# Attention with four sink columns and a gated MLP on one core: sinks of three tiles held as high, low and high parts in 72 rows of f32r

## The chip, the cores and the metric

One core of a Trainium2 chip runs the whole program. The metric is the device time of one execution in microseconds (us); lower is better. The kernel before was timed three times, and the median is what counts. One execution was also taken by the hardware profiler; its instruction records are "the trace" below.

## The reference

Inputs are q, k and v of shape (4, 8, 768, 64) in float32 (batch, heads, sequence, head dimension), four sinks, a window of 128 keys, and the weights of an MLP with 512 inputs and 1024 hidden columns. The attention's output, with its heads side by side, is the MLP's input:

```
scores = q @ k^T / sqrt(64)
keep   = (key < n_sink) or (0 <= query - key < window)
a      = softmax of the kept scores, divided by (sum + 1e-9)
x      = a @ v, heads side by side              # (4, 768, 512)
h      = max(x @ w_in, 0)                       # (4, 768, 1024)
conv   = conv_w[0]*h[s-1] + conv_w[1]*h[s] + conv_w[2]*h[s+1]
out    = (h * sigmoid(conv)) @ w_out            # (4, 768, 512)
```

So each query sees the four sinks, which are the first four keys of its sequence, and the 128 keys that end at itself.

## The kernel before

The sequence is cut into six tiles of 128 queries. A "pair" is two heads of one batch (16 pairs, four to a batch), and a "half" is three query tiles of a pair: 32 halves in all. The main loop in `banded` takes one query tile of one pair as a step (96 steps). A step has three slots: scores and softmax of this tile, the transposes of the tile before (`transp`), and, when that closes a half, the product of probabilities and values for the half (`pv`). Between the slots the loop puts pieces of the MLP of the batch that is already done (`Moe.pieces`: first products at L174, second products at L201), paced so that they are used up when the next batch's attention ends. In the first batch there is no MLP to fill in for the first half of the steps; there the weights are read and split instead (`Moe.narrow` and `Moe.split`, L99 to L113): 64-bit numbers come from memory, are narrowed by four operations into a 32-bit tile, and split into a high part in f32r and the rest. The order of the instructions on each engine is not the program's alone: a scheduler with its own model of time orders them when the kernel is built, and the engines then run their queues in that order.

The band is handled with keys and queries in tiles of 128. The four sinks are handled apart. The probabilities of a step have 132 columns, of which the first four are the sinks' (`pe`). Per half, `transp` does this when its third tile has come (L490 to L495): VectorE copies the first 16 columns of the three tiles and two heads, with only four of them real sinks (`SP = 16`), to `sk` (128 x 96 float32); TensorE turns it (L493) into a PSUM tile `tk` with the tag "h"; ScalarE copies it to `sT` (96 x 128). In `pv` each query tile of the half then gets one product (L515) with `c.vs[:, w]`, a stationary matrix of 96 rows by 128 columns in float32 that holds the sinks' values in the rows of tile w and zeros in all other rows. There are two such products in the first half of a pair (tile 0 needs none) and three in the second; they close the accumulation in `px` which the band's products (L512) began.

`sink_load` fills `c.vs`, once for a batch: six DMAs from memory to the rows of each tile and head, on SP's queue. SP issues every DMA of the kernel, in order. The tile `c.vs` exists once, so a batch's loads wait until the last product of the batch before has read it. The call for the first batch stands ahead of the loop, between the fetches of the first weights and of the first queries and keys; the later ones stand at the third step of a batch. The zeros of `c.vs` are set once by GpSimd (L400).

Tiles with the tag "st" have three buffers of 128 x 512 float32. Before the loop the masks' helpers hold two of them, then each narrowing of weights takes two (`w` and `low`), and at the end of a chunk of the MLP each of two output tiles takes one (L205) until its DMA to memory has landed. The second products collect in PSUM tiles "po", of which there are two.

Of the kernel before, what the change touches and what calls it, by code (L numbers as in the profile page):

```python
# [10 lines left out]
F32 = mybir.dt.float32  # L11
F32R = mybir.dt.float32r
I32 = mybir.dt.int32
AF = mybir.ActivationFunctionType
ALU = mybir.AluOpType
PSUM = bass.MemoryType.PSUM

P = 128
D = 64
NEG = 1.0e9  # L20
NS = 4
SP = 16
KW = P + NS
SW = 2 * P + NS
CH = 256
# [11 lines left out]
def f(ap):  # L37
    return ap.bitcast(F32)
# [304 lines left out]
def load_half(c, g, nm, half, slot):  # L343
    n = c.S // P // 2
    return load(c, g, nm, slot, n * half, n * half + n)
# [5 lines left out]
    return c.v_raw[slot]  # L351


def sink_load(c, b):

    for j in range(2):
        src = c.v[b].rearrange("(g j) s d -> j s g d", j=2)[j, 0:NS]
        for u in range(3):
            r = 2 * SP * u + SP * j
            dst = c.vs[r:r + NS, u].rearrange("s (g j d) -> s g j d", j=2, d=D)[:, :, j]  # L360
            c.nc.sync.dma_start(dst, src)


def banded(c):

    nc = c.nc
    m = Moe(c)
    A = Attn(c, m.x, KW, m.mp, m.ps)
    T = A.T
    NPAIR = c.H // 2  # L370
    NG = c.B * NPAIR
    cp = c.es.enter_context(c.tc.tile_pool(name="bc", bufs=1))
    ap, ps = A.ap, A.ps
# [9 lines left out]
    R, C, inw, sk, tmp, prv = [tmps[i // 3][:, P * (i % 3):P * (i % 3) + P] for i in range(6)]  # L383
# [12 lines left out]
    for mk in (m0, m1, m2):  # L396
        nc.vector.tensor_scalar(mk, mk, -NEG, NEG, ALU.mult, ALU.add)

    c.vs = cp.tile([6 * SP, 3, NPAIR * P], F32, name="vs")
    nc.gpsimd.memset(c.vs, 0.0)  # L400
    c.headscale = cp.tile([P, 2], F32, name="headscale")
    nc.gpsimd.memset(c.headscale, 0.0)
    for j in range(2):
# [5 lines left out]
    st = [Ctx() for g in range(NG)]  # L409
# [18 lines left out]
    def fetch(upto=len(queue)):  # L428

        while free[0] and asked[0] < min(len(queue), upto):  # L430
            free[0] -= 1
            g, nm, half = queue[asked[0]]
            st[g].raw[nm, half] = load_half(c, g, nm, half, c.raw[asked[0] % RAWB])
            asked[0] += 1
# [33 lines left out]
    def keytile(g, kt, hf):  # L468

        s = st[g]  # L470
        if (kt, hf) not in s.pT:
            s.pT[kt, hf] = ap.tile([P, 2, 2, P], F32, tag="pT", name=f"pT{g}_{kt}_{hf}", bufs=PTB)
        return s.pT[kt, hf]

    def transp(g, t):
        s = st[g]
        hf, u = divmod(t, 3)
        pt = pts[:, A.n % 2]
        A.n += 1
        for j in range(2):  # L480
            nc.tensor.transpose(pt[:, j, :], s.pe[hf][:, u, j, NS:KW], c.ident)  # L481
        own = keytile(g, t, hf)[:, :, 0]
        nc.scalar.copy(own, pt)  # L483
        if t:
            nc.gpsimd.affine_select(out=keytile(g, t - 1, hf)[:, :, 1], in_=own, pattern=[[0, 2], [-1, P]],  # L485
                                    compare_op=ALU.is_gt, fill=c.zero, base=0, channel_multiplier=1)
            nc.gpsimd.affine_select(out=own, in_=own, pattern=[[0, 2], [1, P]], compare_op=ALU.is_ge, fill=c.zero,
                                    base=0, channel_multiplier=-1)
        if u == 2:
            pk = m.ps.tile([P, P], F32, tag="h", name=f"tk{g}_{t}", bufs=2)  # L490
            sk = ap.tile([P, 6, SP], F32, tag="sk", name=f"sk{g}_{hf}")
            nc.vector.tensor_copy(sk, s.pe[hf].rearrange("p t h k -> p (t h) k")[:, :, 0:SP])
            nc.tensor.transpose(pk[0:6 * SP, :], sk.rearrange("p t k -> p (t k)"), c.ident)  # L493
            s.sT = ap.tile([6 * SP, P], F32, tag="sT", name=f"sT{g}_{hf}")
            nc.scalar.copy(s.sT, pk[0:6 * SP, :])  # L495

    def pv(g, t):

# [22 lines left out]
    def prep(n):  # L521

        g, half = jobs[n]
        if g >= NPAIR and half:
            return []
        if g >= PLAIN:
            return A.prep(g, st[g], ahead)
        if half == 0 and g % 2 == 0:
            kks.append(f(ap.tile([P, 4, T, KW], F32R, tag="kk", name=f"kk{g}")))
        out = []  # L530
        for h in (half, half + 1)[0:1 + g // NPAIR]:
            out += A.prep32(g, h, st[g], kks[g // 2][:, g % 2], "po" if g < NPAIR and h == 0 else "h", ahead)
        return out

    def values(n):
        g, half = jobs[n]
        if g < NPAIR:
            st[g].v = load_v(c, g, n % 2, *((2, T) if half else (0, 3)))
        elif half == 0:
            st[g].v = load_v(c, g, g % 2)  # L540

    def coming(n):

        last = 2 * NPAIR - 2
        if n < last:
            return [(n + 1, -0.4, 1.8)]
        if n == last:
            return [(n + 1, -0.4, 1.4), (n + 2, 1.4, 5.6)]
        return [(n + 2, -0.4, 5.1)] if n % 2 == 0 and n + 2 < len(jobs) else []

    for x in prep(0):
        x()
    m.fetch(1)
    sink_load(c, 0)
    fetch(4)
    m.fetch(2)
    fetch()
    steps = [(n, g, 3 * half + u) for n, (g, half) in enumerate(jobs) for u in range(3)]
    NST = len(steps)
    NSTB = NPAIR * T  # L560
# [8 lines left out]
    for i in range(NST + D2):  # L569
        if i < NST:  # L570
            n, g, t = steps[i]
            if t % 3 == 0:
                for n1, lo, hi in coming(n):
                    new = prep(n1)
                    todo += [(i + lo + (hi - lo) * (k + 1) / len(new), x) for k, x in enumerate(new)]
            if g >= NPAIR or t % 3 == 2:
                fetch()
            if t == 0 and g and g % NPAIR == 0:
                after = i + 3
            if i == after:  # L580
                sink_load(c, g // NPAIR)
            if n + 1 < len(jobs) and (t % 3 == 2 if n < 2 * NPAIR else t == 3):
                values(n + 1)
        m.need(min(sum(i >= w for w in WHEN), len(m.todo)))
        for slot in range(SLOTS):
            if slot == 0 and i < NST:
                scores(g, t)
            if slot == 1 and 0 <= i - D1 < NST:
                transp(*steps[i - D1][1:])
            if slot == 2 and 0 <= i - D2 < NST:  # L590
                pv(*steps[i - D2][1:])
                if i - D2 + 1 in cuts:
                    while fill:
                        fill.pop(0)()
                    lo, hi, span = cuts[i - D2 + 1]
                    fill = m.pieces(lo, hi)
                    rate = len(fill) / (span - 0.5)
                    acc = 0.0
            acc += rate / SLOTS
            while acc >= 1.0 and fill:  # L600
                fill.pop(0)()
                acc -= 1.0
            while todo and i + (slot + 1) / SLOTS >= todo[0][0]:
                todo.pop(0)[1]()
# [73 lines left out]
def attention_gated_mlp(ctx: ExitStack, tc: tile.TileContext, q, k, v, n_sink, window, w_in, conv_w, w_out, out):  # L678
# [33 lines left out]
    with tc.If(fast == 1) as cmp:  # L712
        with ExitStack() as es:
            c.es = es
            banded(c)
# [32 lines left out]
```

## Time and profile before

| | |
|---|---|
| time of the kernel before, median of 3 | 502.26 us (501.8 to 502.49) |
| the profiled execution: its own time | 501.79 us |
| its span, first to last instruction | 500.1 us |
| TensorE busy | 464.2 us (93%) |
| VectorE busy | 371.2 us (74%) |
| ScalarE busy | 325.3 us (65%) |
| GpSimd busy | 322.6 us (65%) |

The profile's page gives the busy time of each engine over the span. PE is TensorE's products and transposes, PEld its weight loads, DVE VectorE, ACT ScalarE, POOL GpSimd, SP the queue that issues DMAs. The shown duration of a product includes the way through the array, and products overlap; what a product costs is read from the time between its start and the start of the next. In the trace the rows of f32r operations read "f32" as well, but a float32 product with moving data appears as two records of one shape (L515: 160 records for 80 products), an f32r one as a single record.

### The profile page before, as it was taken

The page shows a single profiled execution, that of the slowest core. Times are in us where ns is not written, and L with a number is a line of the kernel's source. Part 1 is how long each engine was busy: PE and PEld are TensorE (multiplying, and loading weights), DVE is VectorE, ACT ScalarE, POOL GpSimd, SP SyncE. Part 2 cuts the span into 40 slices and gives each one's busy share as a digit, 9 for nine tenths or more (in the row PEclk, how much of TensorE's full clock was granted, in tenths as well). Part 3 has the DMA queues.
Part 4 walks back from the last instruction along what each step waited for, and adds up shares of the span by engine and source line. Part 5 has one row for each costly group of instructions (what it writes and reads, how often), then busy time and mean ns, then how long its engine had stood idle before and what let it go on. Part 6 is the DMA issues. An engine that isn't in the chain of part 4 may idle for free.

```text
span 500.1 us, 10541 instructions
## 1 busy us (share of the span) xinstructions
PE 464.2 (93%) x3209; PEld 394.7 (79%) x3209; DVE 371.2 (74%) x1248; ACT 325.3 (65%) x1012; POOL 322.6 (65%) x620
## 2 busy tenths in 40 slices
PE   3778598799999999999999999999999999999994
PEld 2546376588888888889888888898888888999992
DVE  5898988978788888877877768686777674556551
ACT  3977657568766867766766666675766754545542
POOL 2587888985877768684866767494656565344341
PEclk9999879999999999999999999999999999999999
DMA  5948434526133341514141331404020100101011
GB/s 125 259 153 224 151 117 101 126 64 156 40 91 80 92 101 45 141 33 97 43 103 42 87 86 31 126 17 98 21 65 24 42 1 1 44 1 44 4 40 50
DMA packets 85989, 39.58 MB, mean 79 GB/s; under 512 B 79244, under 2 KB 79268, under 8 KB 85924
## 3 DMA queue, kind: packets, MB, share of 16 engines
q1 hardware_dynamic: 85924, 38.82, 29.6%
q8 instruction: 28, 0.46, 0.4%
q14 instruction: 37, 0.30, 0.2%
HBM read 27.65 MB, written 6.29 MB: 68 GB/s over the span
## 4 chain that ended last, share of the span: by engine, by line
PE 79%; DVE 8%; POOL 6%; DMA 2%; issue 2%; ACT 1%; SPq 0%; POOLq 0%; DVEq 0%; ACTq 0%
PE ph L174 26%; PE po L201 26%; PE px L512 8%; PE sc L322 4%; PE px L515 3%; PE pts L481 3%; PE sc L323 3%; POOL pe L466 2%; PE tq L261 2%; PE tk L274 2%; PE sc L319 1%; DVE stm L104 1%; DVE sc L457 1%; DVE t L187 1%; DVE stm L105 1%
## 5 line engine op out<-in xcount | busy, mean ns | idle before, releaser
L201 PE MATMUL po<-woH,g 128*128 128x512 f32 x384 | 143.6, 413 | 1.8 <-POOL g L191 1.8
L174 PE MATMUL ph<-xH,wiH 128*128 128x258 f32 (+1 forms) x384 | 112.1, 292 | 1.6 <-ACT X L240 0.8
L466 POOL TENSOR_SCALAR pe<-pe,sm 128x132 f32<-128x132 f32 (+1 forms) x192 | 84.4, 450 | 39.6 <-DVE sm L464 21.6
L174 PE MATMUL ph<-xL,wiH 128*128 128x258 f32 (+1 forms) x384 | 109.2, 285 | 0.5 <-DVE xL L331 0.5
L174 PE MATMUL ph<-xH,wiL 128*128 128x258 f32 (+1 forms) x384 | 109.3, 285 | 0.0
L461 ACT ACTIVATE pe<-pe,sm 128x132 f32<-128x132 f32 (+1 forms) x192 | 77.4, 405 | 39.4 <-DVE sm L458 37.3
L191 POOL TENSOR_SCALAR g<-t 128x256 fp32r<-128x256 f32 x96 | 40.9, 426 | 78.0 <-DVE t L189 55.2
L201 PEld LDWEIGHTS po<-woH,g 128*128 128x128 f32 x384 | 68.9, 190 | 13.5 <-POOL g L191 2.7
L186 DVE SCALAR_TENSOR_TENSOR t<-hb,cw,t 128x256 f32<-128x256 f32 x96 | 57.5, 598 | 29.1 <-ACT t L185 28.4
L174 PEld LDWEIGHTS ph<-xH,wiH 128*128 128x128 f32 x384 | 73.0, 190 | 6.2 <-ACT sT L495 1.2
L192 POOL TENSOR_TENSOR g<-t,g 128x256 fp32r<-128x256 f32 x96 | 74.1, 772 | 4.8
L201 PE MATMUL po<-woL,g 128*128 128x512 f32 x192 | 76.6, 399 | 0.0
L174 PEld LDWEIGHTS ph<-xH,wiL 128*128 128x128 f32 x384 | 72.9, 190 | 2.3
L174 PEld LDWEIGHTS ph<-xL,wiH 128*128 128x128 f32 x384 | 72.8, 190 | 1.6 <-DVE xL L331 0.7
L188 ACT ACTIVATE t<-t 128x256 f32<-128x256 f32 x96 | 40.1, 417 | 38.1 <-DVE t L187 37.5
L189 DVE SCALAR_TENSOR_TENSOR t<-t,hb 128x256 f32<-128x256 f32 x96 | 46.4, 484 | 18.8 <-ACT t L188 18.2
L457 DVE COPY_PREDICATED sc<-before,sc 128x128 f32<-128x128 int32 x160 | 44.7, 290 | 19.9 <-PE sc L323 17.5
L187 DVE SCALAR_TENSOR_TENSOR t<-hb,cw,t 128x256 f32<-128x256 f32 x96 | 55.9, 582 | 3.4
L181 ACT ACTIVATE hb<-ph 128x258 f32<-128x258 f32 (+1 forms) x96 | 37.1, 386 | 31.8 <-PE ph L174 30.8
L458 DVE CUSTOM_DVE_ANT_0 pe<-sc,m 128x132 f32<-128x132 f32 (+1 forms) x192 | 53.3, 287 | 3.7 <-PE sc L323 2.6
L185 ACT ACTIVATE t<-hb,cw 128x256 f32<-128x256 f32 x96 | 49.2, 512 | 8.2 <-POOL g L192 3.6
L485 POOL TENSOR_SCALAR_AFFINE_SELECT pT<-pT 128x256 f32<-128x256 f32 x80 | 38.5, 481 | 21.6 <-ACT pT L483 20.2
(113 smaller groups left out, 950.2 us busy)
## 6 DMA issues: line engine op xcount, KB each, us to landing
raw<-in_q_dram SPq DMA_DIRECT2D x64, 96.0 KB
raw<-in_k_dram SPq DMA_DIRECT2D x64, 96.0 KB
out_dram<-stm SPq DMA_DIRECT2D x24, 256.0 KB
kk<-kk SPq DMA_DIRECT2D x24, 198.0 KB
vraw<-in_v_dram SPq DMA_DIRECT2D x24, 192.0 KB
wi_0r<-in_moe_w_in_dram SPq DMA_DIRECT2D x2, 512.0 KB
wi_1r<-in_moe_w_in_dram SPq DMA_DIRECT2D x2, 512.0 KB
wi_2r<-in_moe_w_in_dram SPq DMA_DIRECT2D x2, 512.0 KB
```

Source lines behind the costliest of these rows:

```text
L174: nc.tensor.matmul(u.h[:, 0:W], w[:, cc, ff * P:(ff + 1) * P], x[:, cc, t0:t1], start=(i == 0), stop=(i == len(prods) - 1))
L185: nc.scalar.mul(a, prev, cw[:, 0, ff:ff + 1])
L186: nc.vector.scalar_tensor_tensor(out=e, in0=this, scalar=cw[:, 1, ff:ff + 1], in1=a, op0=ALU.mult, op1=ALU.add)
L187: nc.vector.scalar_tensor_tensor(out=a, in0=nxt, scalar=cw[:, 2, ff:ff + 1], in1=e, op0=ALU.mult, op1=ALU.add)
L189: nc.vector.scalar_tensor_tensor(out=a, in0=e, scalar=1.0, in1=this, op0=ALU.add, op1=ALU.mult)
L191: nc.gpsimd.tensor_scalar(u.g[:, 0], a, 1.0, 1.0, ALU.mult, ALU.mult)
L192: nc.gpsimd.tensor_tensor(out=u.g[:, 1], in0=a, in1=f(u.g[:, 0]), op=ALU.subtract)
L201: nc.tensor.matmul(po[:, 0:c.DM], u.g[:, a, tt * P:(tt + 1) * P], w[:, ff, :], start=(ff == 0 and i == 0), stop=(ff == NFF - 1 and i == 2))
L457: nc.vector.copy_predicated(pc[:, KW:SW], before.bitcast(I32), pc[:, 0:P])
L458: nc.vector.tensor_tensor_reduce(out=pe[:, j, cols], in0=pc[:, P:SW][:, cols], in1=mk, op0=ALU.add, op1=ALU.min, scale=1.0, scalar=3.0e38, ...
L461: nc.scalar.activation(pe[:, j, cols], pe[:, j, cols], AF.Exp, bias=sm[:, j:j + 1], scale=-1.0, accum_out=sm[:, 2 + j:3 + j])
L466: nc.gpsimd.tensor_scalar(pe[:, j, cols], pe[:, j, cols], sm[:, 4 + j:5 + j], 1.0, ALU.mult, ALU.mult)
```

## The change

The 96 rows become 72 (`SR = 24` rows for a part, three parts), all in f32r. Of the probabilities only the four real columns are taken. ScalarE copies them, rounded to f32r, into parts 0 and 2 of `sk`; VectorE writes the float32 value less the rounded one into part 1. One f32r transpose turns all three parts, and ScalarE's copy to `sT` stays, now of 72 rows. The values in `c.vs` hold the parts high, high and low against that, so that one product adds high by high, low by high and high by low. The products at L515 keep their text and count, but both operands are f32r, so each is one pass instead of the two records of a float32 product.

`sink_load` now reads the batch's sinks once into a tile of four rows, rounds them on ScalarE, subtracts on VectorE, and puts the parts in place with 18 DMAs from SBUF to SBUF, on SP's queue. Its three tiles (raw, high, low) come from the tag "st" with the three buffers. For the first batch the call moves behind the fetches.

```diff
-SP = 16
+SR = 6 * NS
...
-def sink_load(c, b):
-
-    for j in range(2):
-        src = c.v[b].rearrange("(g j) s d -> j s g d", j=2)[j, 0:NS]
-        for u in range(3):
-            r = 2 * SP * u + SP * j
-            dst = c.vs[r:r + NS, u].rearrange("s (g j d) -> s g j d", j=2, d=D)[:, :, j]
-            c.nc.sync.dma_start(dst, src)
+def sink_load(c, m, b):
+
+
+    raw, hi, lo = (m.mp.tile([P, 512], d, tag="st", name=f"sink{n}{b}", bufs=3)[0:NS] for d, n in ((F32, "r"), (F32R, "h"), (F32R, "l")))
+    c.nc.sync.dma_start(raw.rearrange("s (h d) -> s h d", d=D), c.v[b].rearrange("h s d -> s h d")[0:NS])
+    c.nc.scalar.copy(hi, raw)
+    c.nc.vector.tensor_tensor(out=lo, in0=raw, in1=f(hi), op=ALU.subtract)
+    for u in range(3):
+        for part, val in enumerate((hi, hi, lo)):
+            for j in range(2):
+                r = SR * part + 2 * NS * u + NS * j
+                dst, src = (f(x).rearrange("s (g j d) -> s g j d", j=2, d=D)[:, :, j] for x in (c.vs[r:r + NS, u], val))
+                c.nc.sync.dma_start(dst, src)
...
-    c.vs = cp.tile([6 * SP, 3, NPAIR * P], F32, name="vs")
-    nc.gpsimd.memset(c.vs, 0.0)
+    c.vs = cp.tile([3 * SR, 3, NPAIR * P], F32R, name="vs")
+    nc.gpsimd.memset(f(c.vs), 0.0)
...
         if u == 2:
-            pk = m.ps.tile([P, P], F32, tag="h", name=f"tk{g}_{t}", bufs=2)
-            sk = ap.tile([P, 6, SP], F32, tag="sk", name=f"sk{g}_{hf}")
-            nc.vector.tensor_copy(sk, s.pe[hf].rearrange("p t h k -> p (t h) k")[:, :, 0:SP])
-            nc.tensor.transpose(pk[0:6 * SP, :], sk.rearrange("p t k -> p (t k)"), c.ident)
-            s.sT = ap.tile([6 * SP, P], F32, tag="sT", name=f"sT{g}_{hf}")
-            nc.scalar.copy(s.sT, pk[0:6 * SP, :])
+            pk = m.ps.tile([P, P], F32R, tag="h", name=f"tk{g}_{t}", bufs=2)
+            sk = ap.tile([P, 3, 6, NS], F32R, tag="sk", name=f"sk{g}_{hf}")
+            sinks = s.pe[hf].rearrange("p t h k -> p (t h) k")[:, :, 0:NS]
+            nc.scalar.copy(sk[:, 0:3:2], sinks.rearrange("p (o t) k -> p o t k", o=1).to_broadcast([P, 2, 6, NS]))
+            nc.vector.tensor_tensor(out=sk[:, 1], in0=sinks, in1=f(sk[:, 0]), op=ALU.subtract)
+            nc.tensor.transpose(pk[0:3 * SR, :], sk.rearrange("p a t k -> p (a t k)"), c.identr)
+            s.sT = ap.tile([3 * SR, P], F32R, tag="sT", name=f"sT{g}_{hf}")
+            nc.scalar.copy(s.sT, f(pk[0:3 * SR, :]))
...
     m.fetch(1)
-    sink_load(c, 0)
     fetch(4)
     m.fetch(2)
     fetch()
+    sink_load(c, m, 0)
...
             if i == after:
-                sink_load(c, g // NPAIR)
+                sink_load(c, m, g // NPAIR)
```

## Rows read from the trace of the kernel before

**Rows 1.** Busy time by stretch of the span: the stretch and its length, then busy us and the number of records for PE, PEld, DVE, ACT and POOL, the granted clock of TensorE, the busy share of the DMA engines, and GB/s.

```profile
0.00:60.00 60.00, 40.70 (x225) 27.78 (x225) 49.89 (x186) 43.29 (x133) 39.72 (x78) 0.98 0.70 190
60.00:120.00 60.00, 51.43 (x338) 41.51 (x336) 51.66 (x157) 38.33 (x117) 48.75 (x79) 0.93 0.41 102
120.00:425.00 305.00, 304.41 (x2233) 265.21 (x2232) 232.43 (x837) 209.84 (x685) 205.13 (x418) 1.00 0.26 65
425.00:500.10 75.10, 67.64 (x420) 60.20 (x418) 37.17 (x70) 33.81 (x78) 29.03 (x47) 0.99 0.09 30
```

**Rows 2.** All waits of PE in the stretch from 120 to 425 us: who waited for whom, us in total, times, the longest.

```profile
PE sc L322 <- DVE sm L458: 0.5, 1, 0.5
```

**Rows 3.** The sinks' products alone (L515) in the third of these stretches: PE busy and records, PEld busy and records, clock, DMA share, GB/s.

```profile
120.00:425.00 305.00, 18.59 (x119) 15.55 (x120) 1.00 0.26 65
```

**Rows 4.** PE in order of time, around four runs of the sinks' products: start, us from the first start to the last end, engine, line, what. Two runs behind the band's float32 products (L512), two behind f32r products.

```profile
203.63 0.94 PE L515 MATMUL px<-sT,vs 96*128 96x128 f32 x6
204.33 0.36 PE L174 MATMUL ph<-xH,wiH 128*128 128x258 f32 x1
204.53 0.28 PE L174 MATMUL ph<-xH,wiL 128*128 128x258 f32 x1
204.65 0.28 PE L174 MATMUL ph<-xL,wiH 128*128 128x258 f32 x1
...
215.87 0.71 PE L515 MATMUL px<-sT,vs 96*128 96x128 f32 x4
216.42 0.38 PE L481 MATMUL pts<-ident,pe 128*128 128x128 f32 x2
...
169.81 0.61 PE L515 MATMUL px<-sT,vs 96*128 96x128 f32 x4
170.17 0.36 PE L174 MATMUL ph<-xH,wiL 128*128 128x258 f32 x1
...
228.92 0.83 PE L515 MATMUL px<-sT,vs 96*128 96x128 f32 x6
229.51 0.37 PE L322 MATMUL sc<-kk,X 128*128 128x260 f32 x1
```

**Rows 5.** PE in order of time where f32r products with 128 moving columns stand between f32r products of 512 and 260 columns, and TensorE's weight loads (PEld) of the same moment.

```profile
219.53 0.40 PE L201 MATMUL po<-woH,g 128*128 128x512 f32 x1
219.76 0.22 PE L322 MATMUL sc<-kk,X 128*128 128x128 f32 x1
219.82 0.27 PE L323 MATMUL sc<-kk,X 128*128 128x128 f32 x1
219.94 0.34 PE L322 MATMUL sc<-kk,X 128*128 128x260 f32 x1
220.11 0.28 PE L323 MATMUL sc<-kk,X 128*128 128x260 f32 x1
...
219.77 0.19 PEld L323 LDWEIGHTS sc<-kk,X 128*128 128x128 f32 x1
219.88 0.19 PEld L322 LDWEIGHTS sc<-kk,X 128*128 128x128 f32 x1
```

**Rows 6.** PE in order of time around one float32 transpose of sinks (L493).

```profile
222.83 0.27 PE L493 MATMUL tk<-ident,sk 128*96 128x128 f32 x1
222.86 0.71 PE L201 MATMUL po<-woH,g 128*128 128x512 f32 x2
223.41 0.28 PE L322 MATMUL sc<-kk,X 128*128 128x260 f32 x1
```

**Rows 7.** The sinks' copy (L492) and a narrowing operation with two SBUF inputs (L105), each from the view of its line: shortest, median and longest duration in ns; the L492 copy at 42.72 us with the GpSimd instruction beside it; and its pieces in the chain that ended last, the first and the last of three of over a microsecond.

```profile
L492 DVE COPY sk<-pe x32: 200/406/1376, 20.3 to 416.0; 128x96 f32<-128x96 f32 x32
L105 DVE SCALAR_TENSOR_TENSOR stm<-stm,stm x17: 677/747/1777, 12.4 to 88.5; 128x512 int32<-128x512 int32 x16, 24x128 int32<-24x128 int32 x1
42.72 1.26 DVE L492 COPY sk<-pe 128x96 f32<-128x96 f32 x1 [1.52 <-POOL pe L466]
42.66 1.26 POOL L113 TENSOR_TENSOR woL<-stm,woH 128x512 fp32r<-128x512 f32 x1
20.29 1.27 DVE sk L492
105.62 1.30 DVE sk L492
```

**Rows 8.** Groups of instructions by line: busy us, mean ns. The nearest to ScalarE's new copies, and the new subtractions on VectorE.

```profile
L495 ACT COPY sT<-tk 96x128 f32<-96x128 f32 x32 | 8.2, 257 | 0.7 <-PE tk L493 0.6
L120 ACT COPY cw<-cwt 128x24 f32<-128x24 f32 x1 | 0.2, 151 | 0.0
L464 DVE RECIPROCAL sm<-sm 128x2 f32<-128x2 f32 x96 | 15.5, 161 | 1.9
```

**Rows 9.** The start: SP's queue, the sinks' six DMAs; a key load from the chain that ended last (start, us to landing); the first narrowing on ScalarE (L102).

```profile
9.08 2.25 SPq L361 DMA_DIRECT2D vs<-in_v_dram  x6
7.94 3.47 DMA raw<-in_k_dram
10.39 0.67 ACT L102 ACTIVATE stm<-wi_0r 128x512 f32<-128x512 f32 x1 [0.28 <-DMA wi_0r<-in_moe_w_in_dram]
```

**Rows 10.** The change of batch near 205 us: SP's queue, the sinks' six DMAs of the third batch; and the copy of two finished output tiles on ScalarE (L205).

```profile
205.26 2.28 SPq L361 DMA_DIRECT2D vs<-in_v_dram  x6
207.84 1.07 ACT L205 COPY stm<-po 128x512 f32<-128x512 f32 x2
```

## The prediction, made before the change was run

> **What bounds the kernel now.** I read the busy time by stretch first. From 120 to 425 us TensorE is busy for 304.4 of 305.0 us, at its upper clock level (granted clock 1.00, so 2.4 GHz), while VectorE has 232, ScalarE 210 and GpSimd 205 us of work there [rows 1]. The waits of that stretch agree: one wait of PE, 0.5 us long [rows 2]. What takes work from TensorE here takes time from the kernel, as long as the three other engines, which have 70 to 100 us to spare, don't turn into a new bound. Ahead of 120 us it is different. In the first 60 us PE is busy 40.7 us and VectorE 49.9; in the next 60 us PE has 51.4, VectorE 51.7 and GpSimd 48.8 [rows 1]. There several engines take turns, and time of PE alone is worth only a part. Behind 425 us the MLP's last pieces run, and the change has nothing there.
>
> **What the sinks' products cost, and what they will.** In the bound stretch stand 24 of the 32 halves: 120 weight loads of L515 [rows 3], which is 60 products of two records each, two products in every other half and three in the rest. The shown durations overlap, so I go by starts. Behind the band's float32 products, three products take 0.70 us (203.63 to 204.33) and two take 0.55 (215.87 to 216.42); behind f32r work two take 0.36 (169.81 to 170.17) and three 0.59 (228.92 to 229.51) [rows 4]. In each case the next f32r product is late as well: 204.33 to 204.53 is 0.20 us where the following gap is 0.12 [rows 4]. I charge 0.08 us for this passage from float32 to f32r.
>
> The f32r product of 128 columns that takes their place is in the trace already, in the scores. Two of them and one of 260 columns take 219.76 to 220.11, 0.35 us; 258 columns cost 0.12 by themselves (204.53 to 204.65) [rows 4], so two cost 0.23 and one 0.115. The start-to-start gap of the first two is only 0.06, but their weight loads follow each other at 0.11 us (219.77, 219.88), and the sinks' products need a new stationary matrix each time [rows 5]. So I take 0.115 a product. That the rows fall from 96 to 72 I count at nothing.
>
> Behind band products the passage is paid at the first sinks' product instead of after the last: 0.55 + 0.08 becomes 0.08 + 0.23, a gain of 0.32; 0.70 + 0.08 becomes 0.08 + 0.345, a gain of 0.355. Behind f32r work it goes away: 0.36 + 0.08 becomes 0.23, a gain of 0.21; 0.59 + 0.08 becomes 0.345, a gain of 0.325. The mean of the four is 0.30 us a half, and 24 halves give **7.3 us**. Lower end: 0.21 for every half, 5.0. Upper end: the gap of 0.06 in place of 0.115, which is 2.5 x 0.055 = 0.14 more a half, or 3.3 more in all, 10.6.
>
> The Trainium skill (TensorE: Matmul & The Clock Gate, Back-to-back issue gap) gives some 81 ns for one of a stream of pairs of weight load and 128-column product. By it the gain would be 60 x 0.034 = 2.0 us more. The row shows 115 ns for two such pairs, and I keep the row.
>
> **The transpose.** L493 and two MLP products take 222.83 to 223.41, 0.58 us [rows 6]; an MLP product alone takes 0.23 (219.53 to 219.76) [rows 5]. So the transpose costs some 0.11 now. As f32r it costs between 0.06 and 0.115 [rows 5]: 0 to 1.2 us over 24 halves. I take **0.3 us**, near the lower end, for the load is still there.
>
> **The halves ahead of 120 us.** Eight halves save 8 x 0.30 = 2.4 us of PE. PE decides only part of this stretch; I take a third, **0.8 us** (0 to 2.4).
>
> **The sinks' copy.** VectorE's copy of 96 columns takes 200 ns at best and 1376 at worst; at 42.72 us it takes 1.26 us, start and length those of a GpSimd subtraction beside it. Three such copies of 1.27 to 1.30 us lie on the chain that ended last, all ahead of 120 us [rows 7]. In their place come ScalarE's copy of 48 values, between 151 ns (24 columns) and 257 ns (128), and a subtraction of 24, by the nearest row 161 ns [rows 8]. If GpSimd doesn't hold up the subtraction, each of the three saves 1.28 - 0.2 - 0.16 = 0.9 us, 2.7 together. If it does, each loses the 0.2 us of the copy, -0.6. The narrowing operation with two SBUF inputs also runs up to 1777 ns against a median of 747 [rows 7], so the subtraction isn't safe from this. I take **0.7 us**. The Trainium skill (VectorE: DVE Perf Modes, Two Vector instructions with no wait between them) says that a second SBUF tensor input goes through a read interface shared with GpSimd; the trace agrees by that 1777, and by the rule the term would be at its lower end. In the bound stretch the copy's chain has no waiter that reaches PE [rows 2], and ScalarE's 24 x 0.2 = 5 us more there fall into 95 us of slack [rows 1]: nothing charged. If that cover went, each half would lose up to the 0.2 us.
>
> **The first batch's sinks.** Today six DMAs take 2.25 us of SP's queue, 0.375 each [rows 9]. Afterwards it is 19, or 7.1 us. The raw load may stand near 9 us; a key load issued at 7.94 takes 3.47 us to land [rows 9], so the rounding and the subtraction (each at most 0.75 us: a row of 512 columns takes 0.67 on ScalarE and 0.75 on VectorE [rows 7, 9]) are done by 14. Eighteen DMAs take 6.75 us of SP, and the last lands 3.5 later: about 24.5. Until then the high and low tiles keep two of the three "st" buffers, and a narrowing of weights needs two. The first one starts at 10.39 now [rows 9], so it is 14 us later. Narrowings follow each other at (88.5 - 12.4) / 16 = 4.8 us [rows 7], so three are pushed back, each with three VectorE operations of up to 0.75 us: at most 6.7 us of VectorE work, moved to where it has no room. What softens it: VectorE has attention of later steps to do meanwhile, and the first weights leave SP 2.25 us earlier. I charge **2.5 us** (0 to 6.7), under the middle.
>
> **The later batches.** The DMAs into `c.vs` wait for the last product of the batch before. In the third batch they start at 205.26 [rows 10] and the first user starts at 215.87 [rows 4]. With 18 or 19 issues at 0.38 the queue ends at 212.5, and with 3.5 us to land the last one comes at 216.0: just late. The output tiles at 207.84 [rows 10] may also find no "st" buffer; the stores and the next loads queue behind the sink DMAs on SP, and behind the stores the two "po" tiles. The other MLP pieces cover most of it. I charge 0.4 us at each of three changes of batch, **1.2 us** (0 to 4.5).
>
> **The sum.** 7.3 + 0.3 + 0.8 + 0.7 - 2.5 - 1.2 = 5.4 us. The profiled span of 500.10 us becomes 494.7; the profiled execution lies 1.69 us above its span (501.79), so 496.4; the median of the runs is 0.47 above that execution (502.26), so **496.9 us**.
>
> **The rivals.**
> *The loads don't set the pace* (0.10). If f32r products of different stationary matrices follow at 0.06 us, as the first gap of rows 5 does, it is 3.3 us more: 493.6; with a start that costs nothing, 491.1. Against it speaks the 0.11 between loads. This is also the direction of the skill's 81 ns, 494.9 by that estimate.
> *The gain is given back at the seams* (0.12). If start and batch changes cost their upper ends in part, 2.6 to 6.3 us beyond what I charged, the time is 499.5 to 503.2. For it: the three "st" buffers and the 7 us of SP are plain in rows 9 and 10. Against it: of the 17 narrowings some 13 come after 24 us anyway [rows 7].
> *The start stands still: slower* (0.16). SP issues in order. If the 18 DMAs come to the head of its queue ahead of the queries and keys of the next halves, SP waits for the raw load, ScalarE and VectorE (5 us) and then issues for 6.75: 11.7 us against 2.25, and attention's next halves start 9.4 us later [rows 9]. Then the sum is 7.3 + 0.3 + 0.8 + 0.7 - 9.4 - 2.5 - 1.2 = -4.0, and the time 506.3. It decides from about 5.4 us of standstill on (502.3). Against it: most loads of the first 24 us stand ahead of the new place of the call, and the scheduler can order SP's queue by readiness.
> *The product isn't cheaper* (0.02). If 128 columns in f32r were charged like float32, nothing is won at L515 and the rest costs some 2 us: 504.3. The 0.23 us for two speaks against it [rows 5].
>
> **How the numbers follow.** My forecast, 494.5 to 499.5, has 0.60. A run of this kernel can tell about 0.2% from no change, which is 501.25 to 503.25. Below lie the forecast, the faster rival and half of the second: 0.76. Within: the rest of the second and a little more, 0.07. Above: 0.17. The range from 491 to 505 leaves out the end of the first rival and the worse half of the third, about 0.12; it takes in the bounds of the products (5.0 to 10.6) and the middle of those of the start.
>
> **What would show it.** Right: 80 records at L515 instead of 160, at 0.11 to 0.12 us start to start, with PE still full from 120 us to the end of attention and that stretch some 7 us shorter. Start: the first narrowing after 20 us, and the first MLP product no more than 3 us later than now. Wrong: a wait of PE for DMAs into `vs` or for L205 at a change of batch of over 1 us, a granted clock below the 0.98 and 0.93 of the first two stretches [rows 1] for want of work, or an order of the instructions in which TensorE waits for the longer chain from GpSimd over ScalarE and VectorE to the transpose.

## The result: slower by half a per cent, and the profile after

| | before | changed |
|---|---|---|
| median | 502.38 us (501.69 to 504.4, 6 runs) | 505.17 us (504.81 to 505.94, 6 runs) |
| profiled execution, its own time | 501.79 us | 505.34 us |
| its span | 500.1 us | 503.6 us |

The ratio is 1.0051 with a 95% interval of 1.003 to 1.0071. The forecast was 496.9 us and faster. The direction is wrong, and the time lies 0.17 us above the end of the range. What happened is the third rival, "the start stands still" (506.3 us).

The busy time by stretch, of the changed kernel, in the columns of [rows 1]:

```profile
0.00:60.00 60.00, 37.11 (x186) 24.89 (x186) 41.35 (x157) 37.87 (x114) 31.06 (x68) 0.89 0.59 157
60.00:120.00 60.00, 48.01 (x288) 37.43 (x289) 56.54 (x157) 40.41 (x125) 52.45 (x78) 0.91 0.43 116
120.00:425.00 305.00, 303.58 (x2216) 262.24 (x2216) 240.75 (x866) 218.71 (x731) 211.30 (x426) 1.00 0.28 69
425.00:503.60 78.60, 71.12 (x445) 63.23 (x441) 39.40 (x74) 35.28 (x82) 30.50 (x50) 0.98 0.08 29
```

Against [rows 1], the first 60 us hold 3.6 us less work of PE, 8.5 less of VectorE and 8.7 less of GpSimd, and the DMA share falls from 0.70 to 0.59. The granted clock is 0.89 and 0.91 where it was 0.98 and 0.93. The third stretch is as full as before. At 425 us PE has 71.1 us of work left instead of 67.6, and that is the whole difference of the spans, 3.5 us.

A landmark shows in which stretch the time went. L330 rounds a finished half of attention; the eighth one ends the first batch, the 32nd ends attention. The line view of L330 (shortest, median, longest duration in ns, then the first and the last start in us): the kernel before, up to 120 us and for the whole span.

```profile
L330 ACT CAST xH<-px x8: 454/466/483, 28.4 to 115.7; 128x384 fp32r<-128x384 f32 x8
...
L330 ACT CAST xH<-px x32: 454/478/516, 28.4 to 425.3; 128x384 fp32r<-128x384 f32 x32
```

The changed kernel, up to 125 us and for the whole span:

```profile
L330 ACT CAST xH<-px x8: 462/474/488, 32.3 to 124.5; 128x384 fp32r<-128x384 f32 x8
...
L330 ACT CAST xH<-px x32: 459/482/517, 32.3 to 426.1; 128x384 fp32r<-128x384 f32 x32
```

The first batch ends 8.8 us later (124.5 against 115.7). From there to the end of attention it takes 301.6 us instead of 309.6, which is 8.0 less. The tail takes 77.5 us instead of 74.8, 2.7 more, because more of the MLP is left over (from 425 us on, 434 records at L174 and L201 instead of 417). 8.8 - 8.0 + 2.7 = 3.5 us. The 2.7 us were only moved, so behind the first batch 5.3 us were gained, and the start took 8.8.

The largest change at the start is on SP's queue. SP's issues in order of time, of the changed kernel (start, us, queue, line, what, how many): the raw sinks, the 18 DMAs into `vs`, and the fetch of weights that comes behind them.

```profile
11.62 0.43 SPq L358 DMA_DIRECT2D sinkr<-in_v_dram  x1
...
17.80 2.97 SPq L366 DMA_DIRECT2D vs<-sinkh  x4
20.88 1.32 SPq L366 DMA_DIRECT2D vs<-sinkl  x2
22.24 2.69 SPq L366 DMA_DIRECT2D vs<-sinkh  x4
24.97 1.32 SPq L366 DMA_DIRECT2D vs<-sinkl  x2
26.34 2.69 SPq L366 DMA_DIRECT2D vs<-sinkh  x4
29.07 1.32 SPq L366 DMA_DIRECT2D vs<-sinkl  x2
...
31.58 0.35 SPq L91 DMA_DIRECT2D wi_3r<-in_moe_w_in_dram  x1
```

The same fetch in the kernel before:

```profile
17.91 0.36 SPq L91 DMA_DIRECT2D wi_3r<-in_moe_w_in_dram  x1
```

From 17.80 to 30.39 us SP issues nothing but sinks: 12.6 us. `wi_3r` leaves 13.7 us later. What that does to the other engines stands in ten-microsecond windows, with the columns of [rows 1]. The kernel before, 20 to 30 and 40 to 50 us:

```profile
20.00:30.00 10.00, 8.21 (x48) 5.12 (x47) 9.49 (x44) 9.10 (x34) 7.30 (x17) 1.00 0.78 221
...
40.00:50.00 10.00, 8.44 (x61) 6.28 (x62) 8.41 (x20) 7.80 (x20) 7.47 (x10) 1.00 1.00 258
```

The changed kernel, the same windows:

```profile
20.00:30.00 10.00, 7.27 (x46) 4.88 (x46) 5.68 (x39) 7.39 (x34) 6.51 (x20) 1.00 0.08 15
...
40.00:50.00 10.00, 4.52 (x20) 3.04 (x21) 7.17 (x13) 6.73 (x17) 7.01 (x10) 0.50 0.52 172
```

While SP issues sinks, the DMA engines are all but idle (share 0.08 instead of 0.78), and VectorE runs dry. From 40 to 50 us PE has only 4.5 us of work, and the granted clock is 0.50: the lower level, 1.2 GHz, where it was at 2.4 GHz before. The first narrowing of weights (L102) starts at 17.93 us instead of 10.39, the second at 31.70 instead of 15.27, and the first MLP product (L174) at 53.87 instead of 44.85.

Two kinds of wait point straight at the sinks' DMAs. The second narrowing waits for the last of them (in brackets, how long ScalarE stood idle and what ended it), and TensorE's first products of the sinks wait for them too (2.2 us in total, two waits, the longest 1.1). The changed kernel:

```profile
31.70 0.68 ACT L102 ACTIVATE stm<-wi_1r 128x512 f32<-128x512 f32 x1 [1.04 <-DMA vs<-sinkl]
PE px L522 <- DMA vs<-sinkl: 2.2, 2, 1.1
```

The chain of work that ended last passes over twelve of these issues, 7.7 us, and then over the last DMA itself (start, us, what; the first and the last of the twelve issues):

```profile
21.56 0.64 SPq L366
...
29.07 0.64 SPq L366
29.75 0.66 DMA vs<-sinkl
```

How long one issue holds SP stands in the line views. First the changed kernel's 72 sink DMAs from SBUF to SBUF:

```profile
L366 SPq DMA_DIRECT2D vs<-sinkh x48: 637/638/832, 17.8 to 332.5; - x48
L366 SPq DMA_DIRECT2D vs<-sinkl x24: 637/638/700, 20.9 to 333.8; - x24
```

Then, of the kernel before, its 24 sink DMAs from memory, and another kind that it has too, keys copied from SBUF to SBUF:

```profile
L361 SPq DMA_DIRECT2D vs<-in_v_dram x24: 250/298/667, 9.1 to 318.8; - x24
...
L284 SPq DMA_DIRECT2D kk<-kk x12: 467/467/1172, 93.6 to 373.4; - x12
...
L285 SPq DMA_DIRECT2D kk<-kk x12: 461/546/947, 94.5 to 373.9; - x12
```

The new DMAs hold SP 638 ns each, the old ones 298. The prediction priced the new ones by the old (0.375 us, from the group of six in [rows 9]). The row of the right kind, L284 and L285 at 467 and 546 ns, was in the trace of before and was not used. It would have given 8.4 to 9.8 us of hold for 18: nearer to the 12.6, and still short.

The products did what was forecast. PE in order of time, two sinks' products in the middle of MLP products, and three behind the band's float32 products (L519), of the changed kernel:

```profile
180.42 0.28 PE L174 MATMUL ph<-xH,wiH 128*128 128x258 f32 x1
180.54 0.33 PE L522 MATMUL px<-sT,vs 72*128 72x128 f32 x2
180.72 0.34 PE L174 MATMUL ph<-xH,wiL 128*128 128x258 f32 x1
180.89 0.28 PE L174 MATMUL ph<-xL,wiH 128*128 128x258 f32 x1
...
425.53 0.55 PE L522 MATMUL px<-sT,vs 72*128 72x128 f32 x3
425.92 0.33 PE L174 MATMUL ph<-xH,wiL 128*128 128x258 f32 x1
426.09 0.28 PE L174 MATMUL ph<-xL,wiH 128*128 128x258 f32 x1
```

Two products take 0.18 us to the next start, and the gap behind that is 0.17 instead of 0.12: 0.23 us in all, the prediction's figure. Three behind band products take 0.39 + 0.05 = 0.44 (forecast 0.08 + 0.345). In [rows 4] such runs cost 0.36 + 0.08 and 0.70 + 0.08.

### The profile page after: what moved, and what is told of

Same layout as the page of the kernel before. It is cut to its first block, busy times and chain, and to the rows that moved or that the text cites. A ratio compares the mean times of both kernels' runs of the same rounds, so it can differ in the third digit from the quotient of the medians.

```text
span 503.6 us, 10471 instructions
## 1 busy us (share of the span) xinstructions
PE 459.8 (91%) x3129; PEld 387.8 (77%) x3129; DVE 378.0 (75%) x1252; ACT 332.3 (66%) x1048; POOL 325.3 (65%) x620
## 4 chain that ended last, share of the span: by engine, by line
PE 71%; DVE 12%; POOL 6%; ACT 3%; DMA 3%; issue 2%; SPq 2%; POOLq 0%; ACTq 0%; DVEq 0%
PE ph L174 25%; PE po L201 24%; PE px L519 7%; PE sc L322 3%; PE pts L486 3%; PE sc L323 3%; POOL pe L471 2%; PE tq L261 2%; PE px L522 2%; DVE t L186 2%; SPq L366 2%; DVE stm L105 1%; DVE stm L104 1%; PE tk L274 1%; POOL wiL L113 1%
## 5 line engine op out<-in xcount | busy, mean ns | idle before, releaser
L201 PE MATMUL po<-woH,g 128*128 128x512 f32 x384 | 144.3, 414 | 2.0 <-POOL g L191 1.6
L174 PE MATMUL ph<-xH,wiH 128*128 128x258 f32 (+1 forms) x384 | 111.8, 291 | 2.6 <-ACT X L240 1.3
L174 PE MATMUL ph<-xH,wiL 128*128 128x258 f32 (+1 forms) x384 | 109.2, 284 | 0.0
L174 PE MATMUL ph<-xL,wiH 128*128 128x258 f32 (+1 forms) x384 | 108.9, 284 | 0.0
L466 ACT ACTIVATE pe<-pe,sm 128x132 f32<-128x132 f32 (+1 forms) x192 | 77.5, 405 | 31.0 <-DVE sm L463 29.6
L191 POOL TENSOR_SCALAR g<-t 128x256 fp32r<-128x256 f32 x96 | 42.3, 441 | 81.5 <-DVE t L189 58.2
L186 DVE SCALAR_TENSOR_TENSOR t<-hb,cw,t 128x256 f32<-128x256 f32 x96 | 59.2, 617 | 32.8 <-ACT t L185 31.8
L201 PEld LDWEIGHTS po<-woH,g 128*128 128x128 f32 x384 | 69.4, 190 | 14.6 <-POOL g L191 3.6
L174 PEld LDWEIGHTS ph<-xH,wiH 128*128 128x128 f32 x384 | 72.7, 189 | 8.0 <-ACT X L240 1.5
L201 PE MATMUL po<-woL,g 128*128 128x512 f32 x192 | 76.4, 398 | 0.0
L174 PEld LDWEIGHTS ph<-xH,wiL 128*128 128x128 f32 x384 | 72.7, 189 | 2.3
L174 PEld LDWEIGHTS ph<-xL,wiH 128*128 128x128 f32 x384 | 72.6, 189 | 0.8
L189 DVE SCALAR_TENSOR_TENSOR t<-t,hb 128x256 f32<-128x256 f32 x96 | 47.9, 499 | 15.3 <-ACT t L188 14.5
L187 DVE SCALAR_TENSOR_TENSOR t<-hb,cw,t 128x256 f32<-128x256 f32 x96 | 55.5, 578 | 4.4 <-POOL pT L490 0.5
L462 DVE COPY_PREDICATED sc<-before,sc 128x128 f32<-128x128 int32 x160 | 44.2, 287 | 13.7 <-PE sc L323 9.0
L519 PE MATMUL px<-pT,vraw 128*64 128x256 f32 (+1 forms) x448 | 49.7, 348 | 1.3 <-DVE xL L331 0.6
```

Source lines behind the costliest of these rows:

```text
L174: nc.tensor.matmul(u.h[:, 0:W], w[:, cc, ff * P:(ff + 1) * P], x[:, cc, t0:t1], start=(i == 0), stop=(i == len(prods) - 1))
L186: nc.vector.scalar_tensor_tensor(out=e, in0=this, scalar=cw[:, 1, ff:ff + 1], in1=a, op0=ALU.mult, op1=ALU.add)
L187: nc.vector.scalar_tensor_tensor(out=a, in0=nxt, scalar=cw[:, 2, ff:ff + 1], in1=e, op0=ALU.mult, op1=ALU.add)
L189: nc.vector.scalar_tensor_tensor(out=a, in0=e, scalar=1.0, in1=this, op0=ALU.add, op1=ALU.mult)
L201: nc.tensor.matmul(po[:, 0:c.DM], u.g[:, a, tt * P:(tt + 1) * P], w[:, ff, :], start=(ff == 0 and i == 0), stop=(ff == NFF - 1 and i == 2))
L462: nc.vector.copy_predicated(pc[:, KW:SW], before.bitcast(I32), pc[:, 0:P])
```

## The experiments

Three theories were to be told apart. **A, the queue:** SP issues in order, and 18 slow issues at the start keep the loads behind them waiting. **B, the buffers:** the sinks' tiles keep "st" buffers until their DMAs have landed, and the narrowing of weights waits for these. **C, the hop:** the split of the sinks' probabilities goes from GpSimd over ScalarE and VectorE to the transpose, one engine more than before, and that delays each half. A fourth way is the wait above, of TensorE's products for DMAs into `vs`; no run takes it by itself. Beside the theories stood the question whether the products gained what was forecast. Each ratio is against the kernel before, timed beside the experiment on the same chip (medians 502.04 to 502.92 us).

### Without the first batch's load

```diff
     fetch()
-    sink_load(c, m, 0)
```

> The changed kernel without the first batch's sink load; the sinks of that batch stay zero, so its part of the output is left out of the sum. Theory A (the 18 DMAs from SBUF to SBUF, at 0.64 to 0.68 us of SP each, hold SP from 17.8 to 30.4 us and the start stands): the first MLP product comes back from 53.9 to about 45 us, and the time falls by 8 to 10, to 495 to 497 us. Theory B (the high and low tiles hold two of the three st buffers, so the weights are narrowed late): the same 495 to 497, since both go away. Theory C (the start is long because the sinks' probabilities now pass over ScalarE and VectorE before the transpose): 503 to 505.5, hardly a change.

Measured: 497.94 us, ratio 0.9903 (0.9889 to 0.9918). The first load costs the changed kernel 505.17 - 497.94 = 7.2 us, by the ratios 7.4. With both intervals at their ends it lies between 5.6 and 9.1. The time is a microsecond above what A and B expected and far below what C did. The loss is in the start, then. But not everything returns to what it was. L330 up to 120 us in this kernel:

```profile
L330 ACT CAST xH<-px x8: 461/472/480, 32.6 to 117.9; 128x384 fp32r<-128x384 f32 x8
```

The first batch ends 2.2 us later than in the kernel before, with no sink load in its way at all, and the first MLP product still starts at 53.6 us, not at the expected 45. So that delay of the first MLP product isn't the load's doing.

### The low part in the raw tile's place

```diff
-    raw, hi, lo = (m.mp.tile([P, 512], d, tag="st", ..., bufs=3)[0:NS] for d, n in (...))
+    raw = m.mp.tile([P, 512], F32, tag="st", name=f"sinkr{b}", bufs=3)[0:NS]
+    hi = m.mp.tile([P, 512], F32R, tag="sinkh", name=f"sinkh{b}", bufs=1)[0:NS]
+    lo = raw.bitcast(F32R)
```

> The changed kernel with one of the three tiles (high) in a buffer of its own and the low part written over the raw one, so that the sinks keep one of the three st buffers in place of two; the 18 DMAs stay as they are. Theory A: SP still issues them for 12 us, the time stays at 503.5 to 505.5 us. Theory B: two buffers are free, the second narrowing is back at about 16 us in place of 31.7, and the time falls to 496 to 499 us. Theory C: no change, 505.

Measured: 502.33 us, ratio 0.9989 (0.9975 to 1.0003), 2.8 us less than the changed kernel, 3.1 by the ratios (1.4 to 4.8 with both intervals at their ends). That lies between what A and what B expected. The first narrowings start at 11.74, 15.77 and 22.13 us, so B is real. SP's queue in this kernel:

```profile
16.67 0.42 SPq L91 DMA_DIRECT2D wi_3r<-in_moe_w_in_dram  x1
...
18.75 2.92 SPq L368 DMA_DIRECT2D vs<-sinkh  x4
...
30.52 1.32 SPq L368 DMA_DIRECT2D vs<-sinkr  x2
```

The scheduler has also put `wi_3r` ahead of the sinks' DMAs. So the 2.8 us are not the buffers' alone, all the more as the later batches' sinks hold one buffer less here too; on the other side they still hold one of the three. They are a size for B, some 3 us. What remains of the 7.2 us, some 4, is left for the 18 issues, which still take from 18.75 to 31.84 us, and for TensorE's wait for `vs`, which is 2.6 us here.

### Float32 products again, all else as changed

```diff
-nc.tensor.matmul(px[...], c.vs[:, w, P * hp:P * hp + P], s.sT, ...)
+nc.tensor.matmul(px[...], f(c.vs[:, w, P * hp:P * hp + P]), f(s.sT), ...)
```

> The changed kernel with the products of the sinks read as float32 again (72 rows, all three parts; two records a product); sink loads, split and transposes as changed. Measures the products' gain alone. By my prediction's step (0.115 us in place of 0.2 to 0.23, 0.30 us a half): 24 halves of the bound stretch cost 7 us again, 511.5 to 513 us. If the products gain nothing where it counts: 505.

Measured: 512.48 us, ratio 1.02 (1.0184 to 1.0215). The f32r products are worth 512.48 - 505.17 = 7.3 us in all 32 halves, 7.5 by the ratios, give or take 1.8 with both intervals at their ends. L522 alone in the bound stretch, with the columns of [rows 3]; first this kernel:

```profile
120.00:425.00 305.00, 19.63 (x120) 15.94 (x120) 1.00 0.28 69
```

and the changed one:

```profile
120.00:425.00 305.00, 11.64 (x60) 8.77 (x60) 1.00 0.28 69
```

Half the records and 8.0 us less of busy time (the shown durations overlap, so this is not the gain itself).

### The kernel before with 18 such DMAs on SP

This was to take A by itself: the kernel before, products and sinks untouched, and 18 DMAs of the same shape between rows of a spare tile, behind the fetches ahead of the loop.

```diff
     fetch()
+    spare = m.mp.tile([P, 512], F32, tag="spare", name="spare", bufs=1)
+    nc.gpsimd.memset(spare, 0.0)
+    for i in range(18):
+        dst, src = (spare[r:r + NS].rearrange("s (g j d) -> s g j d", j=2, d=D)[:, :, i % 2] for r in (32 + NS * (i // 2), 0))
+        nc.sync.dma_start(dst, src)
```

> The kernel before with 18 DMAs more on SP, of the new shape (4 rows, 16 pieces of 256 bytes, SBUF to SBUF, between two places of a spare tile that nobody reads), at the changed kernel's place ahead of the loop; nothing else. Theory A: SP stands for some 11 us behind the first fetches and the start is 7 to 9 us late: 509 to 511.5 us. Theories B and C: the st buffers and the sinks' chain are as before, 502 to 503 us.

Measured: 512.23 us, ratio 1.02 (1.0184 to 1.0217), 9.3 us over the kernel before (502.92) and a little more than A expected. SP's queue in this kernel:

```profile
14.09 12.46 SPq L562 DMA_DIRECT2D spare<-spare  x18
```

Nothing waits for these DMAs and they hold no "st" buffer; the tile's memset takes 0.64 us of GpSimd at 8.64 us, with four small memsets behind it and then nothing until 13.9. But the edit did one thing more. The scheduler put a transpose of queries, which waits for a DMA until 11.28 us, ahead of the first scores on TensorE. The first scores of this kernel and of the kernel before:

```profile
11.94 1.06 PE L319 MATMUL sc<-kk,X 128*128 128x128 f32 x4
...
9.69 1.27 PE L319 MATMUL sc<-kk,X 128*128 128x128 f32 x4 [1.29 <-ACT X L240]
```

They come 2.2 us later, before SP's hold begins. So the 9.3 us belong to the hold and this order together. The next run has the same order, and the difference of the two is free of it.

### The same with memory as the source

```diff
         dst, src = (spare[...] for r in (32 + NS * (i // 2), 0))
+        src = c.v[0].rearrange("(g j) s d -> j s g d", j=2)[i % 2, 0:NS]
         nc.sync.dma_start(dst, src)
```

> As the kernel before with 18 DMAs more on SP, but these read v from memory as the six old ones do, in place of SBUF; same place, same target. If the issue of a DMA from SBUF to SBUF is what is long (0.64 us against 0.25 to 0.38 of the old six), SP stands for 5 to 7 us in place of 12.5 and the time is 505 to 508 us against 512.2. If any DMA of this shape holds SP for 0.64 us: 511 to 513.

Measured: 507.88 us, ratio 1.012 (1.0103 to 1.0137), 5.8 us over the kernel before (502.04). SP's queue in this kernel:

```profile
14.12 6.52 SPq L563 DMA_DIRECT2D spare<-in_v_dram  x18
```

The count, the sizes and the place are the same, and the first scores start at 11.96 us, as in the run above. SP is held 6.5 us instead of 12.5, and the loss falls from 9.3 to 5.8, by 3.5 us or, by the ratios, 4.0 (2.4 to 5.7). So for DMAs of this shape the source sets how long an issue takes, and the hold alone costs: some 0.6 to 0.7 us for each microsecond between these two runs. A is shown. At that price 12.6 us of hold are 7.4 to 8.5 us, if the first microseconds cost as much as the last; this is an estimate.

### The first batch's DMAs on GpSimd's queue

```diff
-                c.nc.sync.dma_start(dst, src)
+                (c.nc.gpsimd if b == 0 else c.nc.sync).dma_start(dst, src)
```

> The changed kernel with the 18 DMAs of the first batch issued by GpSimd in place of SP; all other loads as changed. Theory A: SP's next loads come 12 us earlier; if GpSimd can issue them beside its work, the time falls by 3 to 4.5 us (what keeping the tiles costs, about 2.8, stays), to 500.5 to 502 us. If GpSimd's own work, which the start needs too, is held up instead: 504 to 508.

Measured: 509.69 us, ratio 1.0141 (1.0121 to 1.0161), worse than on SP and above both expected ranges. GpSimd in order of time:

```profile
17.18 6.94 POOL L366 DMA_DIRECT2D vs<-sinkh  x12
24.11 3.38 POOL L366 DMA_DIRECT2D vs<-sinkl  x6
```

GpSimd is held 10.3 us (570 ns for one), and its scaling of `pe` stands behind that. PE's waits for it up to 120 us (in total, times, the longest):

```profile
PE pts L486 <- POOL pe L471: 7.1, 5, 5.9
```

The hold only moved to an engine with work of its own.

### The rounding of the probabilities on VectorE

```diff
-nc.scalar.copy(sk[:, 0:3:2], ...)
+nc.vector.tensor_copy(sk[:, 0:3:2], ...)
```

> The changed kernel with the rounding of the sinks' probabilities on VectorE in place of ScalarE; loads and products as changed. Theory A: the chain isn't what makes the start long, 504 to 506 us. Theory C (the extra engine in the chain GpSimd, ScalarE, VectorE, TensorE): 501 to 503.5 us.

Measured: 506.74 us, ratio 1.0075 (1.0058 to 1.0093), 1.6 us over the changed kernel, 1.2 by the ratios, where the two intervals overlap, and a little above what A expected. Taking the hop away doesn't help. But it puts ScalarE's work on VectorE, which the start needs, so a small cost of the hop may be hidden here. That C isn't the main cause is plain from the run without the first load: it has the hop and is 5.0 us faster than the kernel before.

### Without any sink load

```diff
-    sink_load(c, m, 0)
...
-                sink_load(c, m, g // NPAIR)
+                pass
```

> The changed kernel without any sink load; the sinks of all batches stay zero, so their part of the output is left out. Against the run without the first batch's load (497.9 us) this is the price of the three later loads with their 12 us each of SP's queue. If the MLP pieces cover them: 497 to 498.5. If each costs TensorE a microsecond: 494 to 496.

Measured: 496.60 us, ratio 0.9876 (0.9859 to 0.9894). Against the run without the first load the three later ones cost 1.3 us, 1.4 by the ratios; the two intervals just meet, so this is a size, not a sharp number, and it lies between the two expectations. The rest of the change is worth 6.2 us by itself.

### The first batch as before, the others as changed

Here the first batch keeps float32 products of 24 rows and six DMAs from memory, into memory that a later tile of the MLP uses.

```diff
+    if b == 0:
+        for j in range(2):
+            src = c.v[b].rearrange("(g j) s d -> j s g d", j=2)[j, 0:NS]
+            for u in range(3):
+                r = 2 * NS * u + NS * j
+                dst = c.vs0[r:r + NS, u].rearrange("s (g j d) -> s g j d", j=2, d=D)[:, :, j]
+                c.nc.sync.dma_start(dst, src)
+        return
...
+            vs = (c.vs0 if g < NPAIR else c.vs)[:, w, P * hp:P * hp + P]
```

> The first batch's sinks as before (six DMAs from memory at the old place, float32 product and transpose, only the 24 rows and columns that hold something, in memory that the second batch's low part takes over later), the later three batches as changed. Theory A: the start is the old one, first MLP product at about 45 us, and what is left is the gain of the products in the bound stretch, 24 of 32 halves of the 7.3 us that the float32 products cost in the run before: 5 to 6 us under the kernel before, 496.5 to 498 us. If the later batches' loads or the longer chain of the sinks' probabilities eat the gain: 500 to 503.

Measured: 499.51 us (497.52 to 501.54), ratio 0.9937 (0.9914 to 0.9959), between the two expectations; the first MLP product starts at 48.8 us and not at 45. And the same with the low part in the raw tile's place for the later batches:

> As the run above, and for the later batches one tile in a buffer of its own and low over raw, so the sinks keep one of the three st buffers and not two while the vs rows are still read. If output tiles at a change of batch wait for these buffers: 1 to 3 us under the run above; if not, equal within 1 us.

Measured: 497.59 us (497.43 to 498.54), ratio 0.9895 (0.9878 to 0.9913): 5.3 us faster than the kernel before and 7.6 faster than the changed one. It is the fastest kernel here that computes all of the reference. Its busy time by stretch, first and third:

```profile
0.00:60.00 60.00, 43.08 (x219) 30.09 (x219) 45.11 (x184) 41.23 (x126) 39.48 (x75) 0.94 0.68 182
...
120.00:425.00 305.00, 304.00 (x2224) 264.26 (x2225) 238.78 (x852) 216.38 (x724) 209.47 (x422) 1.00 0.27 67
```

The first 60 us hold 43.1 us of PE, 2.4 more than in [rows 1], and the DMA share is back at 0.68. The runs of the first of the two spread over 4 us, so the 1.9 us between them isn't a sure number.

## Why the prediction was wrong

**The step that failed** is "The first batch's sinks", charged at 2.5 us with an upper end of 6.7. It measured 7.2. It failed in two places. The issue was priced by the DMAs that the change removes, from memory, at 0.375 us; the new ones go from SBUF to SBUF and take 0.64, so 18 of them hold SP 12.6 us and not 6.75. And the step looked for the cost in the "st" buffers and the narrowings; the loads that stand behind the 18 issues on SP it put at nothing. The runs show both at work. The step's own wait exists: the second narrowing waits for the last DMA and starts at 31.70 us, where the step had the last landing at about 24.5, because the issues are longer; freeing a buffer brings back some 3 us. And in the kernel before, where the added DMAs hold no buffer, 5.9 us more of hold cost 3.5 to 4.0 us. For the whole 12.6 us that makes an estimate of 7.4 to 8.5, so hold and buffers overlap, and how they share the 7.2 us isn't shown.

**The third rival** had the mechanism and nearly the time, 506.3 against 505.17, with 0.16 of the chance. That its sum comes so near is luck. It charges 9.4 us for the standstill and 2.5 for the buffers, 11.9 together, where 7.2 were measured, and it counts 1.8 us of other gains (0.3, 0.8 and 0.7) that no run shows. Within its standstill two errors cancel. It had SP wait 5 us for the raw sinks, ScalarE and VectorE; in the trace SP issues other loads from 12.15 to 17.7 us while the sinks land and are split (ScalarE from 15.70 us, VectorE from 16.35). And it had 6.75 us of issues where there are 12.6. The reason given against it, that most loads of the first 24 us stand ahead of the call's new place, was true and not enough: 26 of 35 stand ahead of the 18 DMAs in the changed kernel. The nine behind them (`wi_3r`, the next queries and keys and the small weights, which left from 17.91 us on before) left behind the hold.

**The products** were right as a mechanism. 80 single records, 0.23 us for two, no wait of PE worth a name between 120 us and the end of attention. The sum had 7.3 us for the bound stretch and 0.8 for the early halves, 8.1 together; measured are 7.3 for both, give or take 1.8, so the 0.8 between is within the noise, and no run separates the two terms.

**The transpose and the sinks' copy** (0.3 and 0.7 us) have no run of their own. The subtraction's line view in the changed kernel:

```profile
L499 DVE TENSOR_TENSOR sk<-pe,sk x32: 169/184/1001, 22.7 to 419.0; 128x24 fp32r<-128x24 f32 x32
```

Its median is near the 161 ns that it was priced by. The longest, 1001 ns, shows that it can be held up as the prediction feared: at 129.80 us it ends with a GpSimd subtraction (L253) that runs from 129.76 for 1.00 us. All waits of PE from 120 to 425 us, in the form of [rows 2]:

```profile
PE sc L322 <- DVE sm L463: 0.4, 1, 0.4
PE tk L500 <- DVE sk L499: 0.3, 1, 0.3
PE ph L174 <- ACT hb L181: 0.3, 1, 0.3
PE px L519 <- DVE xL L331: 0.2, 1, 0.2
```

So ScalarE's and VectorE's additional work is hidden in the bound stretch, as was said.

**The later batches** were charged 1.2 us and measured 1.3, a size only. Their DMAs, with a few other issues between, hold SP 12 to 15 us at each change (124.44 to 138.3, for one), twice as long as was thought, but PE has the MLP to do and no wait of PE points at them.

**The balance.** -7.3 (products) + 7.2 (first load) + 1.3 (later loads) = +1.2 us. The medians differ by 2.8. The 1.6 us between are not settled. By the ratios they are 1.3, and with the intervals of the four runs at their ends this is 1.3 give or take 2.7, so it isn't clear of nothing. If it is real, it may lie in the first batch, which ends 2.2 us late even without its load, at a granted clock of 0.91 in both of the first stretches (0.98 and 0.93 before). In the first 60 us of that run TensorE waits 2.7 us for the subtraction (L499), where it waited 1.3 for the copy (L492) before. Another order of the start by the scheduler could do it too. Neither was tried by itself.

**The signs that the prediction named** came, but they do not single out the cause. The first MLP product is 9.0 us later instead of at most 3, and the granted clock of the first two stretches is below 0.98 and 0.93. Both stand in the run without the first load as well (53.6 us; 0.91 and 0.91), and that kernel is 5.0 us faster than the one before. The first narrowing was to come after 20 us and came at 17.93. The wait for DMAs into `vs` came in the first batch (two of 1.1 us), not at a change of batch.

## What to carry to other kernels

Price each DMA that a change adds by a row of its own kind, source and destination included, and then read how long its issue holds the queue, not only when it lands: what stands behind it on that queue pays. Here the start had no room for 18 small transfers, while the same transfers in the middle, beside a full TensorE, cost some 0.4 us a batch. So a saving for the bound stretch can be taken there alone, with the first batch left nearly as it was (497.59 us against 505.17). And a run that only adds the suspected cost can change the order of the instructions as well: compare two such runs with each other, and not only with the kernel before.

## What the hardware showed that was not expected

- SP was held 638 ns by a DMA of 4 rows from SBUF to SBUF, and 299 ns by one of the same rows and pieces from memory (18 of each, 12.5 and 6.5 us). On GpSimd's queue it was 570 ns, and GpSimd did no other work in that time.
- With PE busy 5.9 and then 4.5 us of ten, the granted clock in the changed kernel was 0.98 from 30 to 40 us and 0.50 from 40 to 50. So this start, short of work, had idle time and the lower level of the clock as well; no run prices the clock by itself. The kernel before has such a stretch too (0.60 from 60 to 70 us).
